# Keys loaded first, batch 1's queries projected sooner, the first quotient in halves, and stores moved to GpSimd, in a sketched attention followed by a routed expert layer

## The chip, the cores and the metric

The kernel runs on one core of a Trainium2 chip. The metric is the time of one execution in device microseconds, as the median of several. Five engines work side by side and wait for one another by semaphores: TensorE (matmul), VectorE, ScalarE, GpSimd, and SyncE, which only issues transfers. ScalarE and GpSimd can issue transfers as well. In the profile they are PE (PEld for the loading of its weights), DVE, ACT, POOL and SP.

## The reference

Attention with a polynomial sketch gives x, and x goes through an expert layer in which every expert works on every row, with a weight P from eight Sinkhorn steps. Cut to what matters:

```python
def _attn_ref(q, k, v, S1, S2):                  # q, k, v: (4, 4, 1088, 32); S1, S2: (8, 32), float64
    def phi(x):
        a = np.einsum('rd,bhsd->bhsr', S1, x)
        b = np.einsum('rd,bhsd->bhsr', S2, x)
        return np.einsum('bhsi,bhsj->bhsij', a, b).reshape(*x.shape[:-1], r * r)
    q_p, k_p = (phi(q), phi(k))
    kv = np.einsum('bhsf,bhsd->bhfd', k_p, v)
    z = np.sum(k_p, axis=2)
    num = np.einsum('bhsf,bhfd->bhsd', q_p, kv)
    den = np.einsum('bhsf,bhf->bhs', q_p, z)[..., None] + 1e-06
    return (num / den).astype(np.float32)

def _moe_ref(x, w_gate, w1, w2):                 # x: (4352, 128); w1: (8, 128, 1024); w2: (8, 1024, 128)
    ...                                          # P: (4352, 8), eight Sinkhorn steps on exp(x @ w_gate)
    for e in range(E):
        h = np.maximum(x @ w1[e], 0.0)
        ye = h @ w2[e]
        out += P[:, e:e + 1] * ye
```

S1 and S2 are stored as 64-bit floats, which VectorE turns into 32-bit ones by eleven small instructions on their words (L34 to L46).

## The kernel before

The program mixes attention and expert layer: batch 0's attention is done first, as fast as it can be, in a layout of its own; as soon as the first 512 columns of xT exist, TensorE starts the expert layer on them (experts 0 and 1 need no weight yet, their results are kept), and the attention of batches 1 to 3 and the Sinkhorn steps are woven into it (`fill(n)` runs n units of the expert layer between two pieces). The expert layer's second products are done in fewer multiplications with sums of blocks of w2, which GpSimd forms and which are stored to DRAM once and loaded again for the next group of rows.

The loads at the start, in this order on SyncE's queue:

```python
    words = mybir.dt.size(S1.dtype) // 4
    raw = consts.tile([P, 2, words * D], U32, name="raw")
    for n, (s, queue) in enumerate(((S1, nc.sync), (S2, nc.scalar))):
        queue.dma_start(out=raw[:, n], in_=s.bitcast(U32).unsqueeze(0).to_broadcast([P // R, R, words * D]))
...
    warm = aps.tile([P, 512], F32, tag="a", name="a")
    for _ in range(14):
        nc.tensor.matmul(warm[:, 0:P], ones, ones, start=True, stop=True)
...
    load_k(0)
    load_q(0, 0, 16)
    load_v(0)
    load_q(1)
    load_q(0, 16)
...
    nc.sync.dma_start(out=wg[:, 0:E], in_=moe_w_gate)
    first_w = load_w(0, False)
    load_k(1)
    load_v(1)
```

The sums of four blocks of w2 and their store:

```python
    def sums_of_four(e, w2):

        ws = pools[0].tile([P, len(FORMS), FO // 4, H2], F32, tag="ws4", name="ws4")
        if e in stored_four:
            nc.sync.dma_start(out=ws, in_=stored_four[e])
            return ws
...
        c = 0
        for ns, x, y, off in FOURS:
            tc.keep_in_program_order(nc.gpsimd.tensor_tensor(ws[:, c:c + len(ns)], blocks(x), blocks(y),
                                                             op=Alu.subtract if off else Alu.add))
            c += len(ns)
        stored_four[e] = dram.tile([P, len(FORMS), FO // 4, H2], F32, name=f"ws4{e}")
        nc.sync.dma_start(out=stored_four[e], in_=ws)
        return ws
```

The small matrices from S1 and S2 (wd projects the keys, wq and wdq the queries), the turning of keys and queries, and batch 0's chain from queries to the quotient:

```python
    def projections():
        flat = raw.rearrange("p n d -> p (n d)")
        s12 = f64_to_f32(nc, consts, flat, (P, 2 * D)) if words == 2 else flat.bitcast(F32)
        st = consts.tile([P, 2, 32], F32, name="st")
        nc.vector.transpose(out=st.rearrange("p n r -> p (n r)"), in_=s12)
        nc.vector.tensor_tensor(wd, st[:, :, 0:R].unsqueeze(2).to_broadcast([P, 2, H, R]),
                                own.unsqueeze(1).unsqueeze(3).to_broadcast([P, 2, H, R]), op=Alu.mult)
        return st
...
    def transpose_q(b, lo=0, hi=S):
        to = kT if b == 1 else qT
        nc.vector.transpose(out=to[:, lo:hi], in_=loaded["q", b].rearrange("p a d -> p (a d)")[:, lo:hi])
...
                nc.tensor.matmul(banks[i][m][:, 0:n], wqf[sl, m, :], qT[sl, lo:hi], start=True, stop=True,
                                 tile_position=(64 * i, 0))
        for i in range(2):
            nc.scalar.copy(phs[0][:, i, lo:hi], banks[i][0][:, 0:n])
...
    def multiply(c, i):
        lo, hi = chunks[c]
        nc.vector.tensor_tensor(phs[0][:, i, lo:hi], phs[0][:, i, lo:hi], queries.pop((0, c, i)), op=Alu.mult)
...
            nc.tensor.matmul(t[64 * i:64 * (i + 1), 0:n], kvz[:, m, i].rearrange("p h d -> p (h d)"),
                             phs[0][:, i, lo:hi], start=True, stop=True, tile_position=(0, 64 * i))
...
    def divide(c):


        lo, hi = chunks[c]
        n = hi - lo
        nb = n // 32
        pn, pd = (queries.pop((0, c, "pn", m)) for m in range(2))
        rd = wk.tile([P, 512], F32, tag="rd", name="rd")
        nc.vector.transpose(out=rd[:, 0:n], in_=pd[:, 0:n])
        rc = wk.tile([P, 16], F32, tag="rc", name="rc")[:, 0:nb]
        nc.vector.tensor_scalar_add(rc, rd[:, 0:n].rearrange("p (b r) -> p b r", r=32)[:, :, 0], 1e-6)
        nc.vector.reciprocal(rc, rc)
        rd = wk.tile([P, 512], F32, tag="rd", name="rd")
        nc.vector.transpose(out=rd[:, 0:n].rearrange("p (b r) -> p b r", r=32),
                            in_=rc.unsqueeze(2).to_broadcast([P, nb, 32]))
        nc.vector.tensor_tensor(xT[:, lo:hi], pn[:, 0:n], rd[:, 0:n], op=Alu.mult)
```

(L376 and L379 are in `query_products`, L384 in `multiply`, L392 in `fractions`; `chunks` of batch 0's columns are 0 to 512, 512 to 800 and 800 to 1088.) Batch 1 to 3 have their queries projected by `queries_ab` (L426), copied to DRAM and read back repeated (`repeat_a`, `repeat_b`).

The first product of the expert layer, one step c of a block (128 or more rows of h; f is the piece of w1, t one of two tiles of columns of x):

```python
            nc.tensor.matmul(ph[sl], loaded_w[j][0][:, P * f + H2 * s:P * f + H2 * (s + 1)],
                             sources[j][:, lo:hi], start=True, stop=True, tile_position=(0, H2 * s))
...

        def step(c):
            f, t = 2 * q + c // 2, c % 2
            first(k, f, t * n, (t + 1) * n, h[c], k % 2)
```

The order in which it is put together:

```python
                if q == 0:
                    if weighted and 1 <= es.index(e) <= es[0] + 1:
                        weigh_kept(g, es.index(e) - 1)
...
    with tc.manual_schedule(engines={engines.DVE, engines.PE, engines.Activation}):
        st = projections()
        repeated(st)
        halves = ((0, NT // 2), (NT // 2, NT))
        transpose_k(0, halves)
        keys_ab(0, halves)
        transpose_q(0, *chunks[0])
        query_products(0)
        for part_ in range(3):
            keys_products(0, part_)
        keys_sums(0)
        for i in range(2):
            multiply(0, i)
        keys_kept(0)
        transpose_q(1)
        transpose_q(0, chunks[0][1])
        fractions(0, 1)
        queries_ab(1)
        fractions(0, 0)
        query_products(1)
        repeat_a(1)
        repeat_b(1)
        divide(0)
        load_q(2)
    with tc.manual_schedule(engines={engines.DVE, engines.PE}):
        for i in range(2):
            multiply(1, i)
        transpose_k(1)
        load_k(2)
        fill(1.25)
        fractions(1, 1)
        fractions(1, 0)
        fill(0.75)
        divide(1)
        keys_ab(1)
        fill(0.75)
        query_products(2)
```

## Time and profile before

| what | value |
|---|---|
| median of 3 | 919.63 us (919.38 to 920.93) |
| span of the profiled execution | 918.0 us |
| instructions | 18893 |
| VectorE busy | 678.9 us (74%) |
| ScalarE busy | 421.6 us (46%) |
| GpSimd busy | 204.0 us (22%) |
| TensorE's granted clock | full in all 40 slices |
| moved by DMA | 128.15 MB, 140 GB/s on average |

A line of the timeline reads: start in us from the span's start, duration in us, engine, line of the kernel, operation, written tile <- read tiles, shape, count; in brackets the idle time of the engine just before, and what ended it. Instructions of one kind that follow each other are merged, so the duration goes from the first one's start to the last one's end. A matmul of 32-bit floats is recorded as two. "ACTq" and "SPq" are the queues in which ScalarE and SyncE issue transfers: the duration is that of the issue. Of the 918.0 us the weighted part of the expert layer, with one piece of work repeated for each expert and group of rows, takes from 184 to 900 us; the attention and the Sinkhorn steps lie before it.

### The profile page before, as it was taken

How to read it: one execution, taken by the hardware profiler on the slowest of the kernel's cores; microseconds unless marked ns; L12 is line 12 of the kernel's file. 1: busy time of each engine (PE TensorE's matmuls, PEld its weight loads, DVE VectorE, ACT ScalarE, POOL GpSimd, SP SyncE). 2: the span in 40 equal slices, each digit the busy share in tenths (PEclk: the TensorE clock that was granted, in tenths of full speed). 3: DMA queues.
4: the chain of work that ended last, by engine and by line, in shares of the span. 5: the costliest groups of instructions: out<-in, count | busy, mean ns of one | idle time of the engine just before them, and what ended most of it. 6: DMA issues, size and time to landing. Idle time of an engine off the chain costs nothing.

```text
span 918.0 us, 18893 instructions
## 1 busy us (share of the span) xinstructions
PE 911.2 (99%) x7442; PEld 637.4 (69%) x7442; DVE 678.9 (74%) x1173; ACT 421.6 (46%) x915; POOL 204.0 (22%) x212
## 2 busy tenths in 40 slices
PE   9999999999999999999999999999999999999997
PEld 6777544466666677777777777777777655556886
DVE  7678699888776798666975656956567976758665
ACT  3455555554444454444544444544445444445443
POOL 3121100175545421201210010110100243210220
PEclk9999999999999999999999999999999999999999
DMA  9994100213454535534364343454445456453640
GB/s 254 308 273 163 54 1 1 70 64 127 148 150 139 186 119 174 165 110 150 114 185 134 117 143 112 132 187 127 133 122 165 130 170 195 162 166 92 177 153 13
DMA packets 91305, 128.15 MB, mean 140 GB/s; under 512 B 25392, under 2 KB 69504, under 8 KB 86480
## 3 DMA queue, kind: packets, MB, share of 16 engines
q1 hardware_dynamic: 88384, 121.42, 42.7%
q0 software_dynamic: 1600, 5.36, 2.1%
q8 instruction: 58, 0.95, 0.4%
q10 hardware_dynamic: 1232, 0.16, 0.1%
q14 instruction: 31, 0.25, 0.1%
HBM read 107.88 MB, written 19.05 MB: 138 GB/s over the span
## 4 chain that ended last, share of the span: by engine, by line
PE 97%; DVE 2%; ACT 1%; issue 0%; POOL 0%; DVEq 0%; POOLq 0%
PE a L914 51%; PE s L1099 41%; PE a L347 1%; PE a L462 1%; PE a L114 1%; DVE hb L931 1%; PE a L314 0%; PE s L376 0%; PE a L426 0%; PE s L392 0%; DVE cs L602 0%; PE a L496 0%; PE a L392 0%; ACT hb L918 0%; DVE rs L596 0%
## 5 line engine op out<-in xcount | busy, mean ns | idle before, releaser
L914 PE MATMUL a<-xe,w 128*64 128x256 f32 (+1 forms) x2560 | 569.8, 470 | 0.0
L918 ACT ACTIVATE hb<-a 128x256 f32<-128x256 f32 (+4 forms) x408 | 195.0, 480 | 241.5 <-PE a L914 209.3
L914 PEld LDWEIGHTS a<-xe,w 128*64 128x64 f32 x2560 | 263.0, 137 | 50.8 <-issue 1.8
L918 ACT ACTIVATE hx<-a 128x256 f32<-128x256 f32 (+1 forms) x360 | 167.3, 465 | 213.5 <-PE a L914 191.6
L1099 PE MATMUL s<-hb,ws 128*64 128x256 f32 (+3 forms) x1312 | 256.1, 395 | 0.2 <-DVE hb L931 0.2
L1099 PE MATMUL s<-hx,ws 128*64 128x256 f32 x1280 | 233.9, 379 | 0.0
L978 DVE TENSOR_TENSOR hb<-hb 128x512 f32<-128x512 f32 (+1 forms) x204 | 133.5, 664 | 102.8 <-ACT hb L918 98.8
L978 DVE TENSOR_TENSOR hx<-hx 128x512 f32<-128x512 f32 (+1 forms) x204 | 149.8, 744 | 65.0 <-ACT hx L918 60.2
L1099 PEld LDWEIGHTS s<-hb,ws 128*64 128x64 f32 x1312 | 134.9, 137 | 87.8 <-issue 64.5
L678 POOL TENSOR_TENSOR xe<-xT,xe 128x768 f32<-128x768 f32 (+2 forms) x41 | 80.3, 1958 | 481.2 <-DMA xe<-pT 377.0
L1099 PEld LDWEIGHTS s<-hx,ws 128*64 128x64 f32 x1280 | 132.7, 137 | 71.6 <-issue 50.3
L914 PE MATMUL a<-xT,w 128*64 128x416 f32 (+3 forms) x512 | 119.7, 462 | 0.0
L1099 PE MATMUL s<-hb,w 128*64 128x256 f32 (+3 forms) x536 | 114.2, 408 | 0.0
L1099 PE MATMUL s<-hx,w 128*64 128x256 f32 x384 | 76.0, 379 | 0.0
L931 DVE TENSOR_TENSOR hb<-hb 128x416 f32<-128x416 f32 (+7 forms) x84 | 60.7, 723 | 18.0 <-ACT hb L918 14.0
L1099 PEld LDWEIGHTS s<-hb,w 128*64 128x64 f32 x536 | 54.1, 137 | 19.0 <-issue 6.5
L914 PEld LDWEIGHTS a<-xT,w 128*64 128x64 f32 x512 | 48.9, 137 | 25.5 <-issue 15.7
L242 POOL TENSOR_TENSOR ws<-w 128x256 f32<-128x256 f32 (+1 forms) x70 | 60.5, 899 | 8.1 <-DMA w<-in_moe_w_dram 5.2
L931 DVE TENSOR_TENSOR hx<-hx 128x256 f32<-128x256 f32 (+1 forms) x65 | 39.5, 612 | 24.0 <-ACT hx L918 22.8
L1099 PEld LDWEIGHTS s<-hx,w 128*64 128x64 f32 x384 | 40.8, 137 | 6.6
L978 DVE TENSOR_TENSOR pqg<-hb 128x512 f32<-128x512 f32 x68 | 40.5, 637 | 0.0
L978 DVE TENSOR_TENSOR pqg<-hx 128x512 f32<-128x512 f32 x68 | 35.0, 554 | 0.0
(181 smaller groups left out, 485.0 us busy)
## 6 DMA issues: line engine op xcount, KB each, us to landing
w<-in_moe_w_dram SPq DMA_DIRECT2D x82, 512.0 KB, 5.5
ws<-ws SPq DMA_DIRECT2D x34, 1024.0 KB, 5.0
xe<-pT SPq DMA_DIRECT2D x34, 384.0 KB, 4.1
ws<-ws SPq DMA_DIRECT2D x12, 512.0 KB, 3.6
ph<-qa SPq DMA_DIRECT2D x12, 288.0 KB, 4.7
rb<-qb SPq DMA_DIRECT2D x3, 1152.0 KB, 7.2
pb<-pT SPq DMA_DIRECT2D x6, 384.0 KB, 8.3
kx<-in_k_dram SPq DMA_DIRECT2D x4, 544.0 KB, 4.0
```

The lines of the kernel that those rows point to most:

```text
L114: nc.tensor.matmul(warm[:, 0:P], ones, ones, start=True, stop=True)
L242: tc.keep_in_program_order(nc.gpsimd.tensor_tensor(ws[:, c:c + len(ns)], blocks(x), blocks(y), op=Alu.subtract if off else Alu.add))
L347: nc.tensor.matmul(pv[64 * s:64 * (s + 1), i], kp[0:n, H * t + h].rearrange("p i j -> p (i j)"), vx[0:n, slots[h], t, :], start=(t == 0 an ...
L462: nc.tensor.matmul(pn[64 * s:64 * (s + 1), t, 2 * i:2 * i + 2].rearrange("p h d -> p (h d)"), ph[:, i, s, 64 * t:64 * (t + 1)], kvs[b % 2] ...
L678: tc.keep_in_program_order(nc.gpsimd.tensor_tensor(out, x, pb, op=Alu.mult))
L914: nc.tensor.matmul(ph[sl], loaded_w[j][0][:, P * f + H2 * s:P * f + H2 * (s + 1)], sources[j][:, lo:hi], start=True, stop=True, tile_posit ...
L918: nc.scalar.activation(out=out, in_=ph, func=Act.Relu)
L931: nc.vector.tensor_tensor(out, a, b, op=Alu.subtract)
L978: nc.vector.tensor_tensor(out if not isinstance(out, tuple) else places(*out), places(*a), places(*b) if isinstance(b, tuple) else b, op=A ...
L1099: nc.tensor.matmul(sums[g][i][H2 * s:H2 * (s + 1), n * place:n * (place + 1)], w, x, start=c == 1, stop=c == per, tile_position=(0, H2 * s))
```

## The change

It has five parts. S1 and S2 are both loaded by ScalarE's queue, so that batch 0's keys are SyncE's first transfer. The product that makes wd goes from VectorE to GpSimd. Batch 1's queries are turned and projected before batch 0's fractions, and not after the first half of them. Batch 0's first quotient (512 columns) is made in two halves of 256, each with its own transposes, addition, reciprocal and product; so that the expert layer can begin on the first half, its first two blocks are reordered: block 0 does the first tile of columns for four pieces of w1, and block 1 the second tile. The number of units of expert work between the pieces of attention is shifted to fit. Last, GpSimd's own queue issues the stores of the sums of four blocks of w2 (but for expert 1), where SyncE had to stand until GpSimd was done with them, and the kept rows are weighed half an item later.

```diff
--- before.py
+++ after.py
@@ -98,8 +98,8 @@
 
     words = mybir.dt.size(S1.dtype) // 4
     raw = consts.tile([P, 2, words * D], U32, name="raw")
-    for n, (s, queue) in enumerate(((S1, nc.sync), (S2, nc.scalar))):
-        queue.dma_start(out=raw[:, n], in_=s.bitcast(U32).unsqueeze(0).to_broadcast([P // R, R, words * D]))
+    for n, s in enumerate((S1, S2)):
+        nc.scalar.dma_start(out=raw[:, n], in_=s.bitcast(U32).unsqueeze(0).to_broadcast([P // R, R, words * D]))
 
     def starts(tile_, c0, blocks):
 
@@ -243,7 +243,11 @@
                                                              op=Alu.subtract if off else Alu.add))
             c += len(ns)
         stored_four[e] = dram.tile([P, len(FORMS), FO // 4, H2], F32, name=f"ws4{e}")
-        nc.sync.dma_start(out=stored_four[e], in_=ws)
+
+        if e == 1:
+            nc.sync.dma_start(out=stored_four[e], in_=ws)
+        else:
+            tc.keep_in_program_order(nc.gpsimd.dma_start(out=stored_four[e], in_=ws))
         return ws
 
 
@@ -257,7 +261,7 @@
         s12 = f64_to_f32(nc, consts, flat, (P, 2 * D)) if words == 2 else flat.bitcast(F32)
         st = consts.tile([P, 2, 32], F32, name="st")
         nc.vector.transpose(out=st.rearrange("p n r -> p (n r)"), in_=s12)
-        nc.vector.tensor_tensor(wd, st[:, :, 0:R].unsqueeze(2).to_broadcast([P, 2, H, R]),
+        nc.gpsimd.tensor_tensor(wd, st[:, :, 0:R].unsqueeze(2).to_broadcast([P, 2, H, R]),
                                 own.unsqueeze(1).unsqueeze(3).to_broadcast([P, 2, H, R]), op=Alu.mult)
         return st
 
@@ -392,22 +396,23 @@
             nc.tensor.matmul(t[64 * i:64 * (i + 1), 0:n], kvz[:, m, i].rearrange("p h d -> p (h d)"),
                              phs[0][:, i, lo:hi], start=True, stop=True, tile_position=(0, 64 * i))
 
-    def divide(c):
+    def divide(c, parts=1):
 
 
         lo, hi = chunks[c]
-        n = hi - lo
+        n = (hi - lo) // parts
         nb = n // 32
         pn, pd = (queries.pop((0, c, "pn", m)) for m in range(2))
-        rd = wk.tile([P, 512], F32, tag="rd", name="rd")
-        nc.vector.transpose(out=rd[:, 0:n], in_=pd[:, 0:n])
-        rc = wk.tile([P, 16], F32, tag="rc", name="rc")[:, 0:nb]
-        nc.vector.tensor_scalar_add(rc, rd[:, 0:n].rearrange("p (b r) -> p b r", r=32)[:, :, 0], 1e-6)
-        nc.vector.reciprocal(rc, rc)
-        rd = wk.tile([P, 512], F32, tag="rd", name="rd")
-        nc.vector.transpose(out=rd[:, 0:n].rearrange("p (b r) -> p b r", r=32),
-                            in_=rc.unsqueeze(2).to_broadcast([P, nb, 32]))
-        nc.vector.tensor_tensor(xT[:, lo:hi], pn[:, 0:n], rd[:, 0:n], op=Alu.mult)
+        for i in range(0, hi - lo, n):
+            rd = wk.tile([P, 512], F32, tag="rd", name="rd")
+            nc.vector.transpose(out=rd[:, 0:n], in_=pd[:, i:i + n])
+            rc = wk.tile([P, 16], F32, tag="rc", name="rc")[:, 0:nb]
+            nc.vector.tensor_scalar_add(rc, rd[:, 0:n].rearrange("p (b r) -> p b r", r=32)[:, :, 0], 1e-6)
+            nc.vector.reciprocal(rc, rc)
+            rd = wk.tile([P, 512], F32, tag="rd", name="rd")
+            nc.vector.transpose(out=rd[:, 0:n].rearrange("p (b r) -> p b r", r=32),
+                                in_=rc.unsqueeze(2).to_broadcast([P, nb, 32]))
+            nc.vector.tensor_tensor(xT[:, lo + i:lo + i + n], pn[:, i:i + n], rd[:, 0:n], op=Alu.mult)
 
 
 
@@ -924,8 +929,11 @@
         h, ts, (later_h, earlier_h, t13) = hs[k] = room_of(k)
 
         def step(c):
-            f, t = 2 * q + c // 2, c % 2
-            first(k, f, t * n, (t + 1) * n, h[c], k % 2)
+            b, f, t = k, c // 2, c % 2
+            if k < 2:
+
+                b, f, t = c // 2, c % 2, k
+            first(b, 2 * blocks[b][1] + f, t * n, (t + 1) * n, room_of(b)[0][2 * f + t], b % 2)
 
         def less(out, a, b):
             nc.vector.tensor_tensor(out, a, b, op=Alu.subtract)
@@ -1131,9 +1139,8 @@
                     w1, w2, _ = loaded_w[j + 1]
                     w = w1, w2, sums_of_two(items[j + 1][1], w2)
                     loaded_w.update({i: w for i in loaded_w if items[i][1] == items[j + 1][1]})
-                if q == 0:
-                    if weighted and 1 <= es.index(e) <= es[0] + 1:
-                        weigh_kept(g, es.index(e) - 1)
+                if q == 1 and weighted and 1 <= es.index(e) <= es[0] + 1:
+                    weigh_kept(g, es.index(e) - 1)
                 if k == len(blocks) - HELD:
                     kept_to_sums(g)
                 m, step, sums_ = (four if tiles == 3 else two)(k)
@@ -1187,28 +1194,28 @@
         for part_ in range(3):
             keys_products(0, part_)
         keys_sums(0)
+        transpose_q(1)
         for i in range(2):
             multiply(0, i)
         keys_kept(0)
-        transpose_q(1)
         transpose_q(0, chunks[0][1])
+        queries_ab(1)
         fractions(0, 1)
-        queries_ab(1)
         fractions(0, 0)
         query_products(1)
         repeat_a(1)
         repeat_b(1)
-        divide(0)
+        divide(0, 2)
         load_q(2)
     with tc.manual_schedule(engines={engines.DVE, engines.PE}):
         for i in range(2):
             multiply(1, i)
         transpose_k(1)
         load_k(2)
-        fill(1.25)
+        fill(2.2)
         fractions(1, 1)
         fractions(1, 0)
-        fill(0.75)
+        fill(0.4)
         divide(1)
         keys_ab(1)
         fill(0.75)
```

## The prediction

> **What bounds the kernel now.** I read the page's busy times first, then what TensorE waited for, then the timeline. The page says that TensorE is the bound and hardly ever waits:
>
> ```profile
> PE 911.2 (99%) x7442; PEld 637.4 (69%) x7442; DVE 678.9 (74%) x1173; ACT 421.6 (46%) x915; POOL 204.0 (22%) x212
> ...
> PE a L392 <- ACT kvz L362: 0.6, 1, 0.6
> PE s L1099 <- DVE hb L931: 0.2, 1, 0.2
> ```
>
> The second and third lines are from the answer on TensorE's waits (us in total, times, longest). A matmul's end is modelled, so small gaps hide inside "busy"; I look for them as starts that lie further apart than the work between them. Inside the expert layers the distance is fixed. In the timeline of TensorE alone (start, duration, group):
>
> ```profile
> 404.23 1.09 PE L914 MATMUL a<-xe,w 128*64 128x512 f32 x4
> 405.09 0.66 PE L1099 MATMUL s<-hx,ws 128*64 128x256 f32 x4
> 405.52 0.66 PE L914 MATMUL a<-xe,w 128*64 128x256 f32 x4
> 405.95 1.09 PE L1099 MATMUL s<-hx,ws 128*64 128x256 f32 x8
> ```
>
> A pair of 256-column matmuls (a group of x4, as each matmul is recorded twice) takes 0.43 us from start to start, a 512-column pair 0.86 us, with nothing between. What is to be won lies where the spacing is worse: the start. From the timeline of the first 30 us:
>
> ```profile
> 0.74 0.67 ACTq L102 DMA_DIRECT2D raw<-in_S_dram  x1
> 0.74 0.71 SPq L102 DMA_DIRECT2D raw<-in_S_dram  x1
> 1.00 6.26 PE L114 MATMUL a<-ones 128*128 128x128 f32 x28 [1.00 <-POOL own L116]
> 1.51 0.80 SPq L161 DMA_DIRECT2D kx<-in_k_dram  x1
> 3.19 0.20 DVE L34 TENSOR_SCALAR mant<-raw 128x64 uint32<-128x64 uint32 x1 [1.44 <-DMA raw<-in_S_dram]
> 5.58 1.29 DVE L302 STREAM_TRANSPOSE kT<-kx 128x512 f32<-128x512 f32 x2
> 7.19 1.15 PE L314 MATMUL a<-wd,kT 128*64 128x64 f32 x32
> 8.38 1.99 PE L376 MATMUL s<-qT,wq 64*128 64x512 f32 x8
> 10.30 2.46 PE L347 MATMUL a<-v,kp 128*64 128x64 f32 x72
> 13.39 1.08 PE L392 MATMUL a<-ph,kvz 128*64 128x512 f32 x4 [0.63 <-ACT kvz L362]
> 14.55 0.72 DVE L403 STREAM_TRANSPOSE rd<-a 128x512 f32<-128x512 f32 x1 [0.46 <-PE a L392]
> 17.41 1.08 PE L914 MATMUL a<-xT,w 128*64 128x256 f32 x8
> 20.34 1.10 PE L314 MATMUL a<-wd,kT 128*64 128x64 f32 x32
> 22.50 0.86 PE L376 MATMUL s<-qT,wq 64*128 64x288 f32 x4
> 23.29 1.95 PE L914 MATMUL a<-xT,w 128*64 128x256 f32 x16
> ```
>
> The first matmul of the expert layer starts at 17.41; before it TensorE runs its warm-up to 7.2, then batch 0's keys, queries and sums. It stands 0.6 us at 13.39, and loses some 0.5 us between 20.34 and 23.29: L314 and its remainder (1.04), one pair of L914 (0.43) and two 288-column pairs of L376 (0.485 each, by the spacing of such pairs later on) are 2.44 us of work in 2.95.
>
> **What the Trainium skill says.** "Perfetto Trace Analysis", Identifying the Most-Contended Engine, says that matmul occupancy is no measure of the distance to the limit; this trace agrees, since its 99% hides the gaps above. "DMA: Bandwidth & Descriptors", Queues, rings and completion order, says that each DMA engine goes round-robin between the queue rows that have work, packet by packet, so the keys on one row will share the engines with S1 and S2 on the other. In the trace before, S1 and S2 ran alone (all 64 KB between 2.2 and 2.8 us), so it doesn't show the cost. "GPSIMD Engine Reference", Elementwise — side-by-side cycle accounting, has GpSimd at about half of VectorE's speed for a long tensor_tensor; here, on 128x64 with broadcasts, the trace has 0.29 us on GpSimd (L267) beside 0.35 on VectorE (L260), so the moved product costs nothing extra.
>
> **Part by part.**
>
> *Loads.* The keys' transfer is issued at 0.74 instead of 1.51, and every later SyncE load moves up by about 0.75 us. But S2 is now issued behind S1 on ScalarE, 0.67 us later. VectorE converts S1 and S2 (3.19 to 5.19) before it turns the keys, in this order in both kernels, so the earlier keys bring nothing here: S2's delay d decides. With d = 0.67 the conversion ends at 5.86. The product wd (0.28 us on VectorE's path) has gone to GpSimd, so the keys' transposes start at 5.19 + d + 0.06, 0.34 us later than 5.58. Both limits have room: the first half of kT is needed at 7.19 (the warm-up sets that) and was ready at about 6.25; qT was ready at 7.75 and is needed at 8.33, when VectorE starts the products. So d costs nothing up to about 0.9 us, and nearly one for one beyond.
>
> *Queries of batch 1 sooner.* Their six matmuls (L426, 0.98 us, from 14.30 to 15.28) move in front of L392, into the time in which TensorE waited for kvz. VectorE turns these queries at 10.94 (1.22 us) ahead of the two products on ph (1.20), which so end at 13.43. TensorE: sums until about 12.7, L426 to 13.66, by when kvz (13.34) and ph are there; the denominators until 14.58, numerators to 15.49, L376 to 16.7. That is the wait filled: about 0.7 us.
>
> *The first quotient in halves.* Denominators land at 13.66 + 1.08 = 14.74, VectorE starts at 14.82. A half costs, from the durations before scaled from 512 to 256 columns (transposes 0.72 to 0.40, product 0.69 to 0.36) with the same gaps: 0.43 + 0.21 + 0.27 + 0.51 + 0.38 = 1.80 instead of 2.75 us. First half of xT: 16.62. The first expert matmul starts at 16.7, just as L376 ends: 0.7 us before 17.41. The order of blocks 0 and 1 is changed so that four pairs use this half alone: TensorE is fed until 18.44.
>
> *What follows.* The second half, interleaved with two products on ph (0.41 each), ends at 18.93. The fractions of chunk 1 start at 18.7 (0.25 of stall) and end at 19.7, a fifth pair goes to 20.13, then the keys of batch 1, whose transpose on VectorE ends at 20.13: L314 at 20.2 instead of 20.34, with one pair more done. A sixth pair and half of L376 cover the wait for the second quotient (22.3), so L376 ends at 22.85 instead of 23.29, with six pairs done instead of five. Gain there: 0.44 + 0.43 = 0.87 us. After this TensorE is fed in both kernels, and the order of the rest is moved by less than one step.
>
> *Stores of w2's sums, and the weighing of kept rows half an item later.* Six stores of 1 MB go from SyncE, which stood up to 17 us for GpSimd's sums, to GpSimd (about 0.7 to 1.1 us each to issue, from L433 and L437). TensorE doesn't wait for weights or for xe in that stage (its waits are above), and GpSimd is 22% busy. Worth 0.
>
> Sum: -0.87 us, plus an expected loss of some 0.2 us from S2, so -0.7: 918.9 us.
>
> **Rivals.**
> - *S2 falls far behind the keys.* If one packet of S1 or S2 alternates with one of the keys (4352 bytes a partition row), S2 lands with d about 2, then qT is 1.2 to 1.6 us late at L376 and nothing catches up; with the gain of 0.87 the kernel ends near 920.2. For: the shared engines. Against: S2 has only 9 small packets per engine (144 on ScalarE's row, by 16 engines). I give it a third.
> - *VectorE eats the gain.* The halves repeat four small instructions; if the keys' transpose of batch 1 falls behind by 0.6 us, L314 and L376 stand as before and the gain is only that of a pair of matmuls: 919.2.
> - *GpSimd's stores hold back xe.* A DMA issue in GpSimd's order ahead of L678 could make TensorE wait at each of six experts; at 1 us each, 925. Against: L678 is done well ahead of its use, as GpSimd idles 377 us waiting for xe's transfers.
> - *More than thought*: rb's transfer, which held VectorE for 4.56 us before L453 at 32.8, also comes sooner; L462 at 34.04 had only 0.3 us in hand. If spacing improves up to 107 us too: 917.8.
>
> **Range and chances.** Counting work by such spacings against the starts, I find only about 3 us of gaps in the first 36 us (an estimate), so 2% (18 us) is out of reach upwards; only the third rival, several times over, could reach it downwards. The range is the first and the last rival with the spread of the times before (919.38 to 920.93). Predicted 918.9, range 917.7 to 920.2; faster by 2% 0.01, within 2% 0.98, slower by 2% 0.01.
>
> **What would show it.** Right: the first expert matmul near 16.7, L426's line ahead of L392's, no wait for kvz, L376 of chunk 2 ended by 22.9, starts 0.43 us apart at 400 us as before. Wrong: raw lands after 4.1 and the first key matmul starts after 7.3; VectorE's key transpose for batch 1 ends after 20.6; or TensorE waits for xe after 184 us.

## The result, and the profile after

The changed kernel takes **924.08 us** (median of 6, 922.29 to 925.24), the kernel before, timed beside it, 920.24 us (919.38 to 920.93): a ratio of 1.004, with a 95% interval of 1.0027 to 1.0053. It is slower by some 4 us, within 2%, and outside the predicted range of 917.7 to 920.2. The profiled execution spans 922.5 us, 4.5 more than before.

TensorE's share is unchanged. From the page of the changed kernel, busy us, share and instructions of each engine:

```profile
PE 912.5 (99%) x7442; PEld 534.1 (58%) x7442; DVE 685.3 (74%) x1177; ACT 421.4 (46%) x915; POOL 208.8 (23%) x219
```

What TensorE waited for is not. The same view as before the change (us in total, times, longest):

```profile
PE a L318 <- DVE kT L306: 2.6, 1, 2.6
...
PE s L1107 <- DVE hb L986: 0.7, 1, 0.7
PE s L1107 <- DVE hb L939: 0.4, 1, 0.4
```

The wait for kvz is gone, as meant; but TensorE now stands 2.6 us for the first keys, and twice for a product of hb. (Lines have moved: L314 is L318, L376 L380, L347 L351, L392 L396, L426 L431, L914 L919, L1099 L1107, L978 L986 in the changed kernel.) Its timeline at the start:

```profile
0.74 1.30 ACTq L102 DMA_DIRECT2D raw<-in_S_dram  x2
0.74 0.38 SPq L161 DMA_DIRECT2D kx<-in_k_dram  x1
...
6.42 0.20 DVE L34 TENSOR_SCALAR mant<-raw 128x64 uint32<-128x64 uint32 x1 [4.67 <-DMA raw<-in_S_dram]
8.36 1.26 DVE L306 STREAM_TRANSPOSE kT<-kx 128x512 f32<-128x512 f32 x2
9.17 1.98 PE L318 MATMUL a<-wd,kT 128*64 128x64 f32 x32 [2.59 <-DVE kT L306]
...
11.25 2.56 PE L380 MATMUL s<-qT,wq 64*128 64x512 f32 x8
13.74 2.46 PE L351 MATMUL a<-v,kp 128*64 128x64 f32 x72
...
17.16 1.89 PE L396 MATMUL a<-ph,kvz 128*64 128x512 f32 x8
...
20.26 1.95 PE L919 MATMUL a<-xT,w 128*64 128x256 f32 x16
```

The keys are issued first, and S1 and S2 land at 6.4 us where they had landed at 3.2. VectorE then converts them and turns the keys, so TensorE's first key matmul comes at 9.17 and not at 7.19. The key matmuls take 1.98 us in place of 1.15 and the query matmuls 2.56 in place of 1.99; the windows of one microsecond say why (the column before the last two is PEclk, the granted clock):

```profile
core 0: us, PE busy (x) PEld busy (x) DVE busy (x) ACT busy (x) POOL busy (x), PEclk, DMA share, GB/s
9.00:10.00 1.00, 0.83 (x16) 0.86 (x18) 1.00 (x4) 0.00 (x0) 1.00 (x5) 0.51 0.96 355
...
11.00:12.00 1.00, 1.00 (x8) 0.64 (x6) 1.00 (x2) 0.47 (x2) 0.00 (x0) 0.50 0.82 275
```

After standing still, TensorE works at half clock for some 3 us (0.78 from 12 to 13, then full); in the kernel before, PEclk is 1.00 in the same windows. In the expert layer the spacing is what it was: near 408 us, starts at 408.90, 409.76 and 410.19, so 0.86 us after a 512-column pair and 0.43 after a 256-column pair. So I follow the delay, the start of a matmul in the changed kernel less the start of the same one before, at the first expert matmul of each width of piece. It is +2.85 us at the first (256 columns, 17.41 before), +2.86 at 288 columns (35.72), +3.18 at 416 (73.6), +3.68 at 384 (144.0), +3.72 at the first weighted matmul (184.21), and +4.50 at the last one (906.61): **2.85 at the start, 0.33 and 0.50 on the way to 144 us, and 0.8 behind the first weighted matmul**, where the delay jumps near 212 us. Three losses, which the experiments take one by one.

### The profile page after: what moved, and what is told of

It is laid out like the page before. It is cut to its first block, busy times and chain, and to the rows that moved or that the text cites. A ratio compares the mean times of both kernels' runs of the same rounds, so it can differ in the third digit from the quotient of the medians.

```text
span 922.5 us, 18903 instructions
## 1 busy us (share of the span) xinstructions
PE 912.5 (99%) x7442; PEld 534.1 (58%) x7442; DVE 685.3 (74%) x1177; ACT 421.4 (46%) x915; POOL 208.8 (23%) x219
## 4 chain that ended last, share of the span: by engine, by line
PE 91%; DVE 6%; ACT 1%; issue 1%; DMA 1%; ACTq 0%; DVEq 0%
PE a L919 47%; PE s L1107 41%; DVE hb L939 1%; PE a L351 1%; DVE hb L986 1%; DMA raw<-in_S_dram 1%; PE a L467 0%; PE s L380 0%; DVE kept L743 0%; PE a L318 0%; PE a L431 0%; DVE z L743 0%; DVE rs L601 0%; ACT hb L923 0%; DVE p L604 0%
## 5 line engine op out<-in xcount | busy, mean ns | idle before, releaser
L919 PE MATMUL a<-xe,w 128*64 128x256 f32 (+1 forms) x2560 | 519.4, 470 | 0.0
L919 PEld LDWEIGHTS a<-xe,w 128*64 128x64 f32 x2560 | 201.9, 137 | 87.7 <-issue 1.6
L1107 PE MATMUL s<-hb,ws 128*64 128x256 f32 (+3 forms) x1312 | 232.3, 395 | 1.3 <-DVE hb L986 0.7
L986 DVE TENSOR_TENSOR hb<-hb 128x512 f32<-128x512 f32 (+1 forms) x204 | 134.1, 667 | 98.7 <-ACT hb L923 94.3
L1107 PE MATMUL s<-hx,ws 128*64 128x256 f32 x1280 | 206.8, 379 | 0.0
L986 DVE TENSOR_TENSOR hx<-hx 128x512 f32<-128x512 f32 (+1 forms) x204 | 151.8, 754 | 63.0 <-ACT hx L923 58.2
L1107 PEld LDWEIGHTS s<-hb,ws 128*64 128x64 f32 x1312 | 106.1, 137 | 118.0 <-issue 84.3
L1107 PEld LDWEIGHTS s<-hx,ws 128*64 128x64 f32 x1280 | 103.4, 137 | 99.9 <-issue 73.7
L919 PE MATMUL a<-xT,w 128*64 128x416 f32 (+3 forms) x512 | 120.5, 463 | 0.2
L1107 PE MATMUL s<-hb,w 128*64 128x256 f32 (+3 forms) x536 | 107.6, 408 | 0.0
L939 DVE TENSOR_TENSOR hb<-hb 128x416 f32<-128x416 f32 (+7 forms) x84 | 58.0, 691 | 21.1 <-ACT hb L923 18.3
L1107 PE MATMUL s<-hx,w 128*64 128x256 f32 x384 | 68.6, 379 | 0.0
L242 POOL TENSOR_TENSOR ws<-w 128x256 f32<-128x256 f32 (+1 forms) x70 | 57.4, 855 | 37.1 <-PE a L919 37.1
L919 PEld LDWEIGHTS a<-xT,w 128*64 128x64 f32 x512 | 49.0, 137 | 26.1 <-issue 16.4
L1107 PEld LDWEIGHTS s<-hb,w 128*64 128x64 f32 x536 | 46.6, 137 | 23.2 <-issue 7.0
L939 DVE TENSOR_TENSOR hx<-hx 128x256 f32<-128x256 f32 (+1 forms) x65 | 40.2, 622 | 23.6 <-ACT hx L923 21.1
L986 DVE TENSOR_TENSOR pqg<-hb 128x512 f32<-128x512 f32 x68 | 42.4, 663 | 0.0
L1107 PEld LDWEIGHTS s<-hx,w 128*64 128x64 f32 x384 | 33.5, 137 | 11.6
L986 DVE TENSOR_TENSOR pqg<-hx 128x512 f32<-128x512 f32 x68 | 38.0, 597 | 0.0
```

What stands on the lines that cost most here:

```text
L939: nc.vector.tensor_tensor(out, a, b, op=Alu.subtract)
L986: nc.vector.tensor_tensor(out if not isinstance(out, tuple) else places(*out), places(*a), places(*b) if isinstance(b, tuple) else b, op=A ...
L1107: nc.tensor.matmul(sums[g][i][H2 * s:H2 * (s + 1), n * place:n * (place + 1)], w, x, start=c == 1, stop=c == per, tile_position=(0, H2 * s))
```

## Experiments

All runs in one table. The kernel before was timed again beside each set of runs (medians of 920.13 to 920.57 us), so rows are best compared by their ratios; e7 and e8 are one execution each, beside 920.57. One execution of e6, of 1240.93 us at a mean clock of 0.753, is left out. "First", "weighted" and "span" are of the one profiled execution: the start of the first expert matmul in us, the delay of the first weighted expert matmul against the kernel before, and that of the span.

One execution is a rough measure of a start. e4 and e17 have the start of the kernel before, in which the first expert matmul came at 17.41: theirs came at 17.37 and 16.77. e9 and e11 start alike, at 16.81 and 16.31. So differences of half a microsecond in these three columns can be chance; the time from the first key matmul to the first expert matmul varies less (10.22 in the kernel before, 10.43 in both e4 and e17).

| run | median us (n) | ratio to before, 95% interval | first | weighted | span |
|---|---|---|---|---|---|
| after | 924.08 (6) | 1.004, 1.0027 to 1.0053 | 20.26 | +3.72 | +4.5 |
| e1: S1 back on SyncE | 920.74 (13) | 1.0006, 0.9998 to 1.0015 | 16.40 | +0.13 | +0.9 |
| e2: e1, stores on SyncE | 920.02 (13) | 0.9996, 0.9988 to 1.0005 | 16.70 | +0.16 | +0.1 |
| e3: before, S1 and S2 on ScalarE | 923.93 (5) | 1.0038, 1.0025 to 1.0051 | 22.28 | +4.85 | +4.7 |
| e4: before, stores on GpSimd | 920.94 (13) | 1.0008, 0.9999 to 1.0016 | 17.37 | +0.46 | +1.1 |
| e5: after, S1 and S2 on SyncE | 920.76 (12) | 1.0008, 1.0 to 1.0017 | 17.54 | +0.98 | +0.7 |
| e6: after, 25 warm-up matmuls | 923.22 (5) | 1.0029, 1.0016 to 1.0042 | 19.29 | +2.71 | +3.4 |
| e7: after, keys in four transfers | 920.83 (1) | | 16.61 | +0.06 | +1.0 |
| e8: e2, quotient in one piece | 920.76 (1) | | 17.91 | +1.13 | +1.0 |
| e9: e2, weaving as before | 919.86 (13) | 1.0, 0.9992 to 1.0008 | 16.81 | +0.01 | -0.1 |
| e10: e9, 12 warm-up matmuls | 920.14 (13) | 1.0004, 0.9995 to 1.0012 | 16.41 | +0.52 | +0.5 |
| e11: e9, batch 3's queries later | 920.09 (21) | 0.9995, 0.9988 to 1.0001 | 16.31 | +0.15 | 0.0 |
| e12: e11, 12 warm-up matmuls | 919.57 (13) | 0.9989, 0.998 to 0.9997 | 17.27 | -0.12 | -0.1 |
| e13: e7, stores on SyncE | 920.66 (13) | 1.0005, 0.9997 to 1.0013 | 16.88 | +2.16 | +1.8 |
| e14: e12, S1, S2 on ScalarE, keys in four | 920.56 (14) | 1.0002, 0.9994 to 1.001 | 17.80 | +0.98 | +0.8 |
| e15: e12, rb from GpSimd | 919.66 (13) | 0.9996, 0.9988 to 1.0004 | 16.48 | -0.06 | -0.2 |
| e16: e13, rb from GpSimd | 920.35 (21) | 1.0004, 0.9997 to 1.001 | 17.19 | +0.64 | +0.4 |
| e17: e4, a pause behind the store | 919.78 (13) | 0.9992, 0.9984 to 1.0001 | 16.77 | -0.12 | -0.4 |

### The start: S1 and S2 behind the keys

My theory on seeing the trace: ScalarE's small packets of S take turns with SyncE's large ones. Rivals: the loss is the half clock's, or comes from wd on GpSimd and the new order of VectorE's work. **e1** undoes the loads alone:

```diff
-    for n, s in enumerate((S1, S2)):
-        nc.scalar.dma_start(out=raw[:, n], ...)
+    for n, (s, queue) in enumerate(((S1, nc.sync), (S2, nc.scalar))):
+        queue.dma_start(out=raw[:, n], ...)
```

> The changed kernel, with S1 again first on SyncE's queue and S2 alone on ScalarE's, ahead of the keys; all else as changed. Theory A (the loss is S2 landing behind the keys: VectorE begins its conversion at 6.42 instead of 3.19, TensorE then stands 2.6 us, and runs at half its clock until about 12.5): conversion at 3.2, first key matmul at 7.2 or less, first expert matmul near 16.8, and 919.6 to 920.4 us, some 4 us less than the changed kernel; what remains against 919 is the stores on GpSimd. Theory B (the reordered queries and the halves are the loss): the first expert matmul stays after 18 and the time above 922.

**e3** puts the same two lines as in the change, and nothing else of it, into the kernel before:

> The kernel before with one part of the change alone: S1 and S2 both on ScalarE's queue, the keys first on SyncE's. Theory A: conversion begins near 6.4, the first key matmul near 9.5 (wd is still made on VectorE), the clock falls to half until about 12.5, first expert matmul near 20.9, and 923.3 to 924.3 us, 3 to 4 us more than the kernel before. Theory B: within 0.7 us of the kernel before.

The timeline of e1, and that of e3:

```profile
3.20 0.20 DVE L34 TENSOR_SCALAR mant<-raw 128x64 uint32<-128x64 uint32 x1 [1.45 <-DMA raw<-in_S_dram]
...
5.79 1.30 DVE L306 STREAM_TRANSPOSE kT<-kx 128x512 f32<-128x512 f32 x2 [0.58 <-DMA kx<-in_k_dram]
...
6.65 1.19 PE L318 MATMUL a<-wd,kT 128*64 128x64 f32 x32 [0.22 <-POOL wq L271]
```

```profile
6.26 0.20 DVE L34 TENSOR_SCALAR mant<-raw 128x64 uint32<-128x64 uint32 x1 [4.50 <-DMA raw<-in_S_dram]
...
9.40 1.97 PE L314 MATMUL a<-wd,kT 128*64 128x64 f32 x32 [3.19 <-DVE kT L302]
...
11.51 3.73 PE L376 MATMUL s<-qT,wq 64*128 64x512 f32 x8
```

In e3 the same chain stands in a kernel that has nothing else of the change: S at 6.26, TensorE idle for 3.19 us, then the key matmuls (1.97) and the query matmuls (3.73) at half clock. In e1 it is gone: conversion at 3.20, keys' transposes at 5.79, first key matmul at 6.65 and full clock. e1 gives back 3.3 us of the 3.84, e3 costs 3.76 (923.93 against 920.17 for the kernel before beside it). The loads are the first cause; e1's time lies 0.3 us above its expected range. In e1 VectorE waits 0.58 us for the keys, where before, with wd still on VectorE, it did not: this is what loading the keys first was for.

**Why they land late.** The DMA view of the changed kernel from 3.5 to 4.5 us (packets, MB, share; q1 is SyncE's row, q10 ScalarE's):

```profile
q1 hardware_dynamic: 154, 0.29, 79.6%
q10 hardware_dynamic: 147, 0.03, 15.6%
```

The two rows share the engines. Of the 288 packets that S1 and S2 have together, 34 move from 2.5 to 3.5 us beside 79 of SyncE's, these 147 beside 154, and 107 from 4.5 to 5.5 beside 273; in the kernel before, all 144 of ScalarE's row moved between 1.5 and 2.5, with 6 of the other. The Trainium skill ("DMA: Bandwidth & Descriptors", Queues, rings and completion order) has each engine go round-robin between the rows that have work, and drain a whole packet, typically of some 9 to 17 descriptors, before it goes to the other row. The mixed rows agree with turns; the records are not told apart by engine here, so how much of a row goes in one turn isn't shown. Nor do the turns explain everything: no packet of S moved before 3.2 us (2.2 in the kernel before), and after 5.2 us none was left, yet the conversion began at 6.42. **e7** tests the turns by the size of the keys' packets, which become 1,024 and 1,152 bytes in place of 4,352:

```diff
-        nc.sync.dma_start(out=kx, in_=k[b].rearrange("h (s a) d -> (h s) a d", a=SA))
+        x = k[b].rearrange("h (s a) d -> (h s) a d", a=SA)
+        for lo, hi in ((0, 8), (8, 16), (16, 25), (25, SA)) if b == 0 else ((0, SA),):
+            nc.sync.dma_start(out=kx[:, lo:hi], in_=x[:, lo:hi])
```

> The changed kernel, with batch 0's keys loaded in four transfers of 8 or 9 rows of 128 bytes a partition (1024 or 1152 bytes a packet instead of 4352); S1 and S2 still on ScalarE's queue. If each packet of S1 and S2 takes its turn with one packet of SyncE's queue, smaller packets ahead of it let it through sooner: conversion begins at 4.5 to 5.5 instead of 6.42. If the DMA engines share by bytes, it stays at 6.2 to 6.6.

```profile
3.84 0.20 DVE L34 TENSOR_SCALAR mant<-raw 128x64 uint32<-128x64 uint32 x1 [2.08 <-DMA raw<-in_S_dram]
```

The conversion starts at 3.84 and the first key matmul at 6.84, sooner than I had expected from turns alone, and the loss at the start is gone. In the window from 2.5 to 3.5 us 190 packets of ScalarE's row moved in place of 34. But in four pieces the keys are also issued later (from 0.74 to 2.80 us, in place of 0.74 to 1.12), so that smaller packets and fewer bytes standing ahead of S aren't told apart here. **e5** sends S1 and S2 through SyncE's row ahead of the keys (`nc.scalar` becomes `nc.sync` in that line), where nothing takes turns:

> The changed kernel with S1 and S2 both on SyncE's queue, one behind the other, and the keys behind them. It tells apart why S2 is late. Theory A1 (it shares the DMA engines with the keys, one packet of each in turn): alone on its queue and ahead of the keys, S2 comes only one issue later, VectorE converts from 3.6 to 4.0, the first key matmul starts by 7.3, and the time is that of S on two queues, 920.7, within 0.6 us. Theory A2 (a second transfer on the same queue is what is slow): conversion begins after 5, TensorE stands over 1 us, time above 922.

```profile
3.71 0.20 DVE L34 TENSOR_SCALAR mant<-raw 128x64 uint32<-128x64 uint32 x1 [1.96 <-DMA raw<-in_S_dram]
```

The conversion starts at 3.71, so a second transfer in one row, issued 0.67 us later, costs about what I had taken S2 to cost (0.5 us beside 3.19). What made S late in the changed kernel is not the second issue but the large transfer beside it.

**e6** separates the clock: 25 warm-up matmuls in place of 14 keep TensorE busy to 8.6 us.

> The changed kernel with 25 warm-up matmuls instead of 14, so that TensorE is busy until about 9 while S2 comes. It measures what of the loss is the clock that falls to half, apart from the lateness. Theory: S2 still lands near 6.4 and the first key matmul starts at 9.2 to 9.7, but runs in 1.2 us instead of 1.98 and the first query products in 2.0 instead of 2.56: 1.0 to 1.6 us less than the changed kernel, 922.5 to 923.1. Rival: the lateness alone costs all of it, and this is no faster than 923.8.

```profile
9.54 1.19 PE L318 MATMUL a<-wd,kT 128*64 128x64 f32 x32 [0.94 <-DVE kT L306]
...
12.77 2.46 PE L351 MATMUL a<-v,kp 128*64 128x64 f32 x72
```

The key matmuls took 1.19 us, at full clock. From the first of them to the first L351 are 3.23 us, where the changed kernel has 4.57 (9.17 to 13.74): the half clock cost 1.34 us there. The median falls by 0.86, a little less than expected; the late landing keeps the rest. The Trainium skill ("TensorE: Matmul & The Clock Gate", Part 1) has the clock halved after an idle window of about 3.4 us; here a stand of 2.6 us was enough, the clock being down from 9.0 us, 2.4 us after the last warm-up matmul (6.58). Stands of 0.94 (e6) and 1.56 us (e14) left it full.

It does not happen each time. By the windows above, the half clock takes 1.71 us of full clock out of 922.5, which would leave a mean of 0.998. Two of the six executions of the changed kernel have 0.999, and took 922.29 and 922.89 us; the other four, at 0.996 to 0.998, took 923.92 to 925.24. How long TensorE stood in those two is not on record.

### Near 212 us: what TensorE waits for with GpSimd's stores

In this stretch GpSimd multiplies x by an expert's weight, which gives xe ("the weighing"); the expert's first product goes to the buffers hb and hx, where VectorE adds and subtracts pieces ("the products" of the lines below) before TensorE's second product.

**e2** adds to e1 the stores of before (one line, `nc.sync.dma_start(out=stored_four[e], in_=ws)`), **e4** puts the change's stores alone into the kernel before:

> As the run before, and the stores of w2's sums back on SyncE's queue. Theory C (a store issued by GpSimd stretches a product on VectorE to 2.8 us near 212 us, for which TensorE stands 1.0 us): 0.7 to 1.2 us less than with the stores on GpSimd, so 918.8 to 919.3, below the kernel before by about 0.9 us, as the prediction summed up for the rest of the change. Rival: the stores are free, and this equals the run before within 0.4 us.

> The kernel before with another part alone: the six stores of w2's sums on GpSimd's queue. Theory C: one or more of VectorE's products take over 2 us beside such a store, TensorE stands 0.5 to 1.2 us in all between 184 and 320 us, time 920.7 to 921.4. Rival: as the kernel before within 0.4 us.

e2 is 0.72 us below e1, e4 0.77 above the kernel before beside it (920.17). So the size is as expected, but e2 stays above its 918.8 to 919.3, and e4's interval just reaches 1. The traces show one place: TensorE stands there for hb in after, e1, e4, e6 and e7, and not in e2. From the first weighted matmul to the last, the delay grows by 0.76 to 0.92 us in those five, and in none of the other traces (-0.39 to -0.01). The timelines of the kernel before, and of e4, at that place:

```profile
208.82 1.41 DVE L978 TENSOR_TENSOR hb<-hb 128x512 f32<-128x512 f32 x2
...
214.21 2.92 DVE L978 TENSOR_TENSOR hx<-hx 128x512 f32<-128x512 f32 x2
214.47 2.12 POOL L678 TENSOR_TENSOR xe<-xT,xe 128x768 f32<-128x768 f32 x1 [6.12 <-DMA xe<-pT]
```

```profile
209.12 0.60 POOL L249 DMA_DIRECT2D ws<-ws  x1 [0.30 <-POOL ws L242]
209.29 3.55 DVE L981 TENSOR_TENSOR hb<-hb 128x512 f32<-128x512 f32 x2
209.73 1.82 POOL L681 TENSOR_TENSOR xe<-xT,xe 128x768 f32<-128x768 f32 x1
...
212.17 0.65 PE L1102 MATMUL s<-hb,ws 128*64 128x256 f32 x4 [0.65 <-DVE hb L981]
```

The expectations above take the store's issue for the cause. But the weighing of xe (L681) starts right behind it; in the kernel before, it waited 6.12 us for its transfer, which SyncE issues behind the store, and fell beside hx. Whichever products of VectorE stand beside the weighing take 1.4 to 2.1 us longer: two of them 3.55 in e4 and 2.92 in the kernel before, where two without it take 1.41. **e17** puts 20 small memsets between e4's first store and the weighing:

```diff
             tc.keep_in_program_order(nc.gpsimd.dma_start(out=stored_four[e], in_=ws))
+            if not idle.get("done"):
+                idle["done"] = True
+                for _ in range(20):
+                    tc.keep_in_program_order(nc.gpsimd.memset(idle["tile"], 0.0))
```

> e4 (the kernel before with the stores on GpSimd) with a pause of 20 small memsets (about 1.8 us) on GpSimd between the first store and the weighing that follows it. Theory (not the store's issue holds VectorE's hb product, but the weighing of xe, L681, which no longer waits for its transfer once SyncE doesn't stand for the sums, and so starts right behind the store, beside a product that TensorE needs next): the weighing starts near 211.5 us, the two hb products beside the store take 1.4 to 1.8 us in place of 3.55, TensorE doesn't wait at the hb of L981, and 920.1 to 920.4 us. Rival (the store's issue itself holds VectorE): the products stay above 2.5 us, TensorE waits 0.6 us, and 920.7 us or more.

```profile
208.52 0.60 POOL L251 DMA_DIRECT2D ws<-ws  x1 [0.30 <-POOL ws L244]
208.69 1.41 DVE L987 TENSOR_TENSOR hb<-hb 128x512 f32<-128x512 f32 x2
...
213.14 2.10 POOL L687 TENSOR_TENSOR xe<-xT,xe 128x768 f32<-128x768 f32 x1
213.48 2.30 DVE L987 TENSOR_TENSOR hx<-hx,pqg 128x512 f32<-128x512 f32 x1
```

The pause took 4.06 us, not 1.8. Beside store and memsets the two products take 1.41 us, to the hundredth what they take in the kernel before; the weighing then stretches a product of hx to 2.30 (0.69 before, at 213.61), for which TensorE doesn't wait; nor does it wait at this hb. So the store's issue doesn't hold VectorE: moved off SyncE, it lets the weighing start beside the product that TensorE needs next. The time is 0.3 us below the expected range, which these lines don't explain; that execution also started its expert layer 0.6 us before e4's. The Trainium skill ("SBUF — State Buffer", SBUF: two separate sides) says that a VectorE operation with two inputs in SBUF and a GpSimd operation that reads SBUF exclude one another; the trace agrees, the products being held for about the weighing's time. e5 has the same stores and no such wait: there the store came at 211.44, after the hb products had ended (210.83), and the weighing stretched four hx products (3.97 us in place of 2.15).

### Between 36 and 144 us: the weaving, and where a lead goes

Nine traces keep the changed weaving (after, e1, e2, e5 to e8, e13, e16). In every one the delay grows by 0.31 to 0.33 us between 35 and 73 us and by 0.47 to 0.50 between 73 and 144, whatever it was at the start. From the first 288-column matmul to the first weighted one TensorE has the same 1363 matmuls in 149.35 us, both in after and in e2, and in the kernel before in 148.49. The wait `L1107 <- hb L939` above comes later, at 164.42 us; it is 0.45 us, and 0.18 at the same place in the kernel before, so that it explains 0.27 us at most. What the rest is made of isn't shown. **e9** turns one number back, the last `fill(0.5)` ahead of the attention loop, to -0.1, which restores the order of before from there on:

> S on two queues, stores on SyncE, queries sooner and halves as changed, but one fill before the attention of batch 1 is cut from 0.5 to -0.1 units, so that from the 24th row on TensorE's and VectorE's instructions stand in the same order as in the kernel before. Theory D (the start does gain 0.7 us, and the shifted weaving gives it back between 55 and 144 us, where VectorE's attention work comes ahead of sums that TensorE waits for): the lead of 0.7 us at the first 288-column block holds to the end, 919.3 to 919.7, against 920.17 before. Rival: the start's gain is lost anyway where VectorE is full, and the time is 920.0 or more.

In the six kernels with e9's weaving (e9 to e12, e14, e15) the delay at 144 us is that at 73, to 0.02 us; in e9 it is 0.04 at 73 and 0.03 at 144. So by these marks the weaving costs 0.8 us. In e9's time it doesn't show (1.0 of the kernel before, where e2 has 0.9996), because e9's lead of 0.6 us was gone by 51 us: there TensorE came to batch 3's queries before VectorE had turned them:

```profile
45.73 4.18 DVE L936 TENSOR_TENSOR hb<-hb 128x576 f32<-128x576 f32 x3 [0.44 <-ACT hb L920]
46.21 0.74 POOL L204 TENSOR_TENSOR ws<-ws,w 128x256 f32<-128x256 f32 x1
```

VectorE is again beside sums of GpSimd; it turned the queries at 49.83 to 51.13, and TensorE, whose matmul before had started at 50.77, took them at 51.28. So I tried to keep the lead: **e10** with a shorter warm-up (12), **e11** with batch 3's queries one piece later, **e12** with both:

```diff
+            yield 1.4
+            keys_products(b + 1, 2)
             ...                                   # batch 3's queries_ab, repeat_a
-            yield 1.4
-            keys_products(b + 1, 2)
```

> As the run before, with 12 warm-up matmuls instead of 14, since the keys are turned at 6.3 and TensorE's warm-up lasts to 7.1. If the warm-up is what holds the first key matmul: up to 0.5 us less, 918.8 to 919.4. If the clock needs the longer warm-up: the first key matmuls run at half the clock (near 2 us instead of 1.15), and the time is the same as with 14 or up to 1 us more.

> As with the weaving put back, and the projection of batch 3's queries one piece later. There the start's lead of 0.6 us was lost in one place: TensorE stood 0.52 us at 51 for the turned queries of batch 3, because VectorE's three differences at 45.7 took 4.18 us beside GpSimd's sums of w2 instead of about 2. If that wait is what eats the lead: no extra there, the lead of 0.5 to 0.7 us at 55 and at 74 us, and 919.4 to 919.7. Rival: the lead goes at the next full place of VectorE, and the time is 919.8 or more, as before the move.

> As the run before with 12 warm-up matmuls, with which the first expert matmul started at 16.41. If the lead can be kept: 919.0 to 919.6, the fastest here. Rival: leads above half a microsecond are stopped by transfers or by VectorE in any order, and it is within 0.3 us of the run with 14.

In their profiled executions e10 and e11 started the expert layer a full microsecond early and stood for it later, each time at the attention of a next batch, whose inputs were not ready: starts lie 0.74 us apart at 37.1 and 0.54 at 51.3 in e10, 1.18 at 33.0 in e11. Both missed their range. e12 met its own and is the only one of the sixteen intervals that lies below 1, but its profiled execution had a lead of only 0.14, so that its tenth of a per cent may be chance. **e13** and **e14** asked whether keys first pays once its packets are small: in the changed kernel with the stores back on SyncE (e13), and with all repairs (e14):

> The changed kernel without its two losses: batch 0's keys in four transfers, so that ScalarE's S1 and S2 take turns with small packets, and the stores back on SyncE. Theory (the loss at the start is the turn-taking with large packets, the loss at the end is GpSimd's stores): the first conversion of S at about 3.9 us, the first key matmul at 7.0 us or before and at full clock, no wait of L1107-like pieces for an hb after 200 us, and 919.6 to 920.0 us. Rival (keys first costs something else besides): 920.2 us or more.

> Batch 0's keys in four transfers ahead of S1 and S2 on ScalarE, stores on SyncE, the weaving of the kernel before, batch 3's queries one piece later, 12 warm-ups. Theory (the keys' landing bounds the first key matmul once the diagonals are on GpSimd, so keys first helps when its packets are small): first key matmul at 6.5 to 6.9 us in place of up to 7.5, and 918.9 to 919.5 us. Rival (the start's lead is absorbed later whatever its size): within 0.3 us of e12's 919.57.

Neither did what I expected. In e14's execution S landed at 5.25 us (3.84 in e7 and e13, 4.64 in e16 below) and the first key matmul came at 8.05, so that small packets don't make sure of it. In e13's the start was good, and 1.4 us were lost at batch 1's first attention matmul:

```profile
35.18 1.83 DVE L457 TENSOR_TENSOR ph<-ph,rb 128x768 f32<-128x768 f32 x2 [6.18 <-DMA rb<-qb]
...
36.24 0.92 PE L466 MATMUL a<-kvs,ph 128*64 128x66 f32 x24 [1.25 <-issue]
```

"issue" hides the releaser: the matmul needs ph, whose product waited for rb. In the other traces this product starts between 30.42 (e2) and 36.70 us (e3). The DMA engines are full at that time: in windows of 4 us their share is 0.81 to 1.19 in the kernel before from 4 to 56 us. **e15** and **e16** let GpSimd issue rb as soon as qb is there, in e12 and e13:

```diff
-        nc.sync.dma_start(out=rb, in_=queries.pop(b)[1]...)
+        x = queries.pop(b)[1]...
+        if b == 1:
+            tc.keep_in_program_order(nc.gpsimd.dma_start(out=rb, in_=x))
+        else:
+            nc.sync.dma_start(out=rb, in_=x)
```

> e12 with one transfer moved: the repeat of batch 1's b's (rb) is issued by GpSimd when qb has landed, no longer by SyncE behind the four repeats of the a's. Theory (the start's lead is given back where the first times product of batch 1 waits for rb, which lands at 30.4 to 35.2 us in the runs, behind a queue that keeps the DMA engines full from 4 us on): the first times product starts at 31 us or before, TensorE does not wait at the first attention matmul of batch 1, the lead at the first 288-column matmul is as large as at the first expert matmul, and 919.0 to 919.5 us. Rival (the bytes set the landing, whatever the queue): rb and the a's land together no sooner, the product at 32 us or after, 919.5 us or more.

> e13 with the same transfer moved. In e13 the first times product waited for rb till 35.18 us and TensorE stood 1.4 us for it. Theory: no such wait, and 919.6 to 920.1 us in place of e13's 920.66. Rival: the wait stays, within 0.3 us of e13.

The timeline of e15:

```profile
32.61 1.83 DVE L459 TENSOR_TENSOR ph<-ph,rb 128x768 f32<-128x768 f32 x2 [3.71 <-DMA ph<-qa]
```

rb was issued at 24.45, once qb had landed (e12: 25.42). The wait at the first attention matmul was absent in both runs (in e12 too), but the product came no sooner than 32.6, now held by the repeats of the a's; and e15 gave 0.6 us of its lead away at batch 1's keys. Times and starts are those of e15's rival, that a move to another queue brings the inputs no sooner; e16 lies between its theory and its rival. Whether the bytes ahead set the landing was not tested, nor whether all inputs of the first 55 us can be brought forward.

**e8** makes the first quotient in one piece again (`divide(0)` in e2):

> S on two queues and stores on SyncE, queries sooner, but the first quotient in one piece. It parts the 0.71 us that the first expert matmul gained (17.41 to 16.70). Theory: the halves are worth most of it, so the first expert matmul starts at 17.4 to 17.7, as TensorE waits for VectorE after the query products; of the lead at the first 288-column block (35.01 against 35.72) some 0.2 to 0.4 us remain, as the filled wait is kept. Rival: the halves bring nothing and it starts at 16.8 or sooner.

```profile
17.91 1.95 PE L916 MATMUL a<-xT,w 128*64 128x256 f32 x16 [0.99 <-ACT ph L380]
```

From the first key matmul to the first expert matmul it has 10.69 us (7.22 to 17.91), e2 9.63 (7.07 to 16.70), the kernel before 10.22. The halves are worth 1.06 us there, and 0.84 at the first 288-column matmul (36.00 against 35.01, less the 0.15 by which e8 began later). That is more than expected: no lead is left at the first 288-column matmul (35.72 in the kernel before). With the quotient in one piece, the queries sooner fill the wait for kvz, but TensorE stands 0.99 us ahead of the expert layer instead. In this one execution they gain nothing without the halves.

## Why the prediction was wrong

*Loads: this step failed.* "With d = 0.67 the conversion ends at 5.86": d was 3.23 us (6.42 less 3.19), because S1 and S2 both shared the DMA engines with the keys' packets. The formula was right: keys' transposes at 5.19 + d + 0.06 = 8.48, measured 8.36. I had given the mechanism a third as a rival, but with d about 2 and only S2 in it, and argued against it by counting S2's 9 packets per engine without asking how long the other row's turns take. The end of the step, "nearly one for one beyond", lacked the clock: 1.98 us of delay at the first key matmul, 3.44 at the first L351, because TensorE came back from its stand at half speed.

*Queries sooner and the first quotient in halves: right,* once the loads are undone. In e2 the lines stand as predicted, without a wait for kvz:

```profile
12.57 1.20 PE L428 MATMUL a<-kT,wdq 128*64 128x192 f32 x12
13.60 1.89 PE L393 MATMUL a<-ph,kvz 128*64 128x512 f32 x8
...
16.70 1.95 PE L916 MATMUL a<-xT,w 128*64 128x256 f32 x16
```

Predicted were 12.7, 13.66, and the first expert matmul at 16.7. From the first key matmul to the first expert matmul e2 is 0.59 us shorter than the kernel before, where 0.7 was predicted. The two parts were not each to be credited as the prediction has it: e8 suggests that the filled wait alone brings nothing and the halves bring all of it. The queries' move was not run alone.

*What follows: right to 35 us, then wrong.* L376 of chunk 2 ended at 23.04 in e2 (predicted 22.85), and the gain at the first 288-column matmul was 0.71 us, not 0.87. "After this TensorE is fed in both kernels, and the order of the rest is moved by less than one step" failed: the shifted weaving costs 0.8 us in every trace that has it, and where it is turned back, most of the lead is taken by inputs that are not there yet.

*Stores: near on the cost of the issue (0.60 us, where 0.7 to 1.1 was predicted), wrong on "Worth 0".* The rival feared that the stores would hold xe back. They did the opposite: xe came sooner, and its weighing met a product of hb. Cost about 0.7 us in the median (e2 and e4), 0.8 in the trace of after.

*The sum.* Predicted -0.7. Of the +3.84 measured, 3.3 are the loads with the half clock (e1), 0.7 the weighing (e2); the start's gain and the weaving's loss cancel within the noise, which is why e2 is at 0.9996. What was on record as "wrong if" came true in its first clause: raw landed after 4.1, the first key matmul after 7.3.

## What to carry to other kernels

A small transfer that everything waits for should be alone on its engines, or ahead in the row of the large one: beside a large one in another row, S landed 3.2 us later here, and TensorE paid once more in clock. Work moved off a queue releases whatever stood behind it there, so look where the released work lands: here beside the one VectorE product that TensorE needed next. A lead won at the start can be lost wherever a later input doesn't come sooner too (here at 33, 37 and 51 us), so follow it through the whole trace by fixed marks before counting it.

## What the runs showed of the hardware that was not expected

- Two rows shared the DMA engines, in one microsecond with 147 small packets beside 154 larger ones. The same transfer of S landed 3.2 us later beside packets of 4,352 bytes; beside packets of about 1 KB 0.65 later in e7 and e13, 1.45 in e16, and 2.1 in e14.
- A stand of 2.6 us was enough, in the profiled execution, for half clock over the next 3 us or so (PEclk 0.50 to 0.51 from 9 to 12 us), and one of 3.19 in e3 for some 7 us (0.62 from 8 to 9, 0.50 to 15, 0.97 from 15 to 16).
- GpSimd's issue of a 1 MB store (0.60 us) and its memsets left VectorE's two-input products alone (1.41 us for two), while its own two-input product of 768 columns stretched one of VectorE's from 0.69 to 2.30 us.
- A 128x60 memset on GpSimd took 0.2 us from start to start (4.06 us for 20), twice the 0.09 us between two 128x64 memsets at the start of the kernel before.
